# Moving table columns, scalings, sines and FFT pieces within the steps of a fused FFN and spectral-gate gradient kernel

## The chip, the core and the metric

The kernel runs on one core of a Trainium2 chip. The metric is the time of one execution on the device, in microseconds. A core has five engines that run their own instruction queues side by side and wait for each other through semaphores: TensorE (PE in the profile; its weight loads are shown as PEld), VectorE (DVE), ScalarE (ACT), GpSimd (POOL) and SyncE (SP, which here only issues DMAs). TensorE writes its sums to PSUM, and VectorE or ScalarE copies them out.

## The reference

The forward pass mixes two branches with a gate; the kernel computes its output and all gradients.

```python
def _fwd_reference(A_x, A_w_r, A_w_i, B_x, B_w_gate, B_w_up, B_w_down, gate_w):
    def _A_ref(x, w_r, w_i):            # x: 1 x 2048 x 576
        X = rfft2(x); X = X * (w_r + 1j * w_i)
        return irfft2(X, s=(2048, 576)).astype(bfloat16)
    def _B_ref(x, w_gate, w_up, w_down):  # 576 -> 4608 -> 576
        return (_gelu(x @ w_gate) * (x @ w_up)) @ w_down
    x = A_x
    g = _sigmoid((x * gate_w).sum(-1, keepdims=True))
    return g * _A_ref(x, A_w_r, A_w_i) + (1 - g) * _B_ref(x, B_w_gate, B_w_up, B_w_down)

def reference(A_x, A_w_r, A_w_i, B_w_gate, B_w_up, B_w_down, gate_w, B_x, grad_out):
    _out, _vjp = jax.vjp(_f, A_x, A_w_r, A_w_i, B_w_gate, B_w_up, B_w_down, gate_w)
    return (_out, *_vjp(grad_out))
```

(The FFT calls are shown shortened, and `_f` is the forward pass with `B_x` held fixed.) The eight outputs are the mixed output, the gradient of x, of the two spectral weights, of the three FFN weights and of the gate's weights. Inputs and outputs are bf16.

## The kernel before

The kernel has two phases. The first is a loop over 18 groups g of 256 hidden features, each with four steps m of 512 of the 2048 rows; step number pr = 4g + m runs from 0 to 71. The second phase (L1151 and around it) multiplies the stored hidden activations and gradients with the FFN weights.

A step of the first phase does this:

- **H work.** `H_mm` computes z (the output's gradient times w_down, L402 and L407), then the gate and up products xy (L411, L418) in two halves; `fft_next` may be called inside the second half, after 11 of its 16 matmuls. ScalarE scales z into da (`H_da`, L430) and copies each half of xy out three ways (`H_act`: xb L439, hu L440, q L437). VectorE does three operations in `H_ew1` (L445 to L447). Then `sigs`, which is `H_ew2`, does two sigmoids on ScalarE (om L461, s L462) and eight operations on VectorE (L466 to L473), whose results are A, dHg and dHu. The sigmoids of the four steps of group 0 are held over and issued in the next step (`held`).
- **W work**, the weight gradients of the group before (`W_units`): pieces called tail (L544, 32 half-width matmuls), dwd (L508) and dw (L527) accumulate in one of two PSUM banks of pool pw, and each ends with a copy (L486) to an output tile by `wcopy`, either on ScalarE (AC) or on VectorE (VC). In step 4 the first parts of two dw pieces run; in step 5 their second parts, the tail and one dwd; in step 7 one dw in four jobs. The dwd pieces read dB, the output's gradient, after it has been scaled in place by 1 - g (`scale_dB`, L952, eight rows of tiles in step 4 and eight in step 5).
- **FFT pieces.** The spectral branch is cut into a list of pieces that `fft_next` takes in order: u1 (L574), u2 (L591), then `tail_table` and `turned` (L608 to L633), s2 (L683), s1 (L772), z, ztail and d of the inverse (L818, L830, L844 and L846). `want` says how many pieces a step takes: none in steps 0 to 5, three in step 6, two in step 7, then one to five. The first goes between the two parts of xy, the others between the W jobs at the places in `spots`. Each piece's matmuls go to the pool pz, which holds one buffer and is shared with z; a ScalarE copy takes them out.

Each engine executes its queue in the order in which the program issues. The FFT needs tables: D (`build_D`), R (`build_R`, four calls for four parts) and B (`columns_B`, `build_B`). VectorE and GpSimd make the arguments; the sines are put in the list `tb.late` and `run_late` issues them on ScalarE, where the sine and sigmoid functions need different tables, so each batch has two table loads around it. Before the loop, tiles of the inputs are transposed on TensorE (`titems`, L367, L370, L373) into PSUM tiles of pool pg or ph, and copied out (L374) as dOT, wdT and xT. `gate` (L383, L385) makes g and 1 - g for a group of rows.

The lines of steps 4 to 71 that place this work:

```python
                if pr in (4, 5):
                    scale_dB(T // 2)
                if pr == 4:
                    build_R(nc, tb, unit, 4)
                elif pr == 5:
                    columns_B(nc, tb, res)
                    next(makeB)
...
                spots = (0.0, 1.6, 3.6) if n < 4 else (0.0, 1.0, 2.6, 4.2, 5.0, 5.0)
                tables = pr in (5, 7)
                for w, f in carry + hs:
                    if k < n and at >= spots[k - (n == 2)]:
...
                    if tables and k == n:
                        run_late(tb)
                        wcopy[0] = VC
```

Of the kernel before, what the change touches and what calls it, by code (L numbers as in the profile page):

```python
# [9 lines left out]
ACT = mybir.ActivationFunctionType  # L10
ALU = mybir.AluOpType
# [9 lines left out]
P, T = 128, 16  # L21
# [135 lines left out]
def build_R(nc, tb, unit, t0):  # L157

    V = nc.vector
    n = 4  # L160
    step = 2.0 * math.pi / S * EPS_SCALE
    X = unit([n, P], I32, name="XR")
    for t in range(n):
        V.scalar_tensor_tensor(X[:, t, :], tb.kk[:, 0, :], tb.scol[:, t0 + t:t0 + t + 1], tb.kk[:, 1, :], op0=ALU.mult, op1=ALU.add)
    V.tensor_single_scalar(X[:], X[:], S - 1, op=ALU.bitwise_and)
    if t0 % 8 == 0:
        tb.Rpair = unit([8, P], name="Rt")
    o = tb.Rpair[:, t0 % 8:t0 % 8 + n, :]

    tb.late.append(lambda: nc.scalar.activation(o, X[:], ACT.Sin, bias=tb.pi[:], scale=-step))  # L170
    tb.Rt += [tb.Rpair[:, t0 % 8 + t, :] for t in range(n)]
# [73 lines left out]
def kernel(  # L245
# [4 lines left out]
    nc = tc.nc  # L250
    LD = nc.sync
    ST = nc.gpsimd
    V = nc.vector
# [3 lines left out]
    res = ctx.enter_context(tc.tile_pool(name="res", bufs=1))  # L257
# [19 lines left out]
    xn = res.tile([P, T, D], BF16, name="xn")  # L277
# [8 lines left out]
    wts = {}  # L286
# [72 lines left out]
    def titems(src, dst, t0, ps, copies, n=4):  # L359

        def item(k, cs):
            def f():
                tp_ = ps[k](BF16).rearrange("p (j t m) -> p j t m", j=2, t=4)
                for j, c in enumerate(cs):
                    for tt in range(n):
                        if c < 4:
                            nc.tensor.transpose(tp_[:, j, tt, :], src[:, t0 + tt, eo(c)], ident[:])  # L367
                        elif n < 4:
                            for r in (LO, HI):
                                nc.tensor.transpose(tp_[r, 0, tt, :], src[:, t0 + tt, 512:D], ident[:])  # L370
                        else:
                            c0 = (t0 + tt) * D + (512, D - P)[tt % 2]
                            nc.tensor.transpose(tp_[:, 0, tt, :], src[:].rearrange("p t d -> p (t d)")[:, c0:c0 + P], ident[:])  # L373
                copies[k](dst[:, cs[0]:cs[0] + len(cs), t0:t0 + n, :], tp_[:, 0:len(cs), 0:n, :])  # L374
            return f
        return [item(k, cs) for k, cs in enumerate(((0, 1), (2, 3), (4,)))]
# [50 lines left out]
    def H_da(g, m, z):  # L427
        da = ewt("da", g)
        for t in range(4):
            nc.scalar.activation(da[:, t, :], z[:, t % 2, t // 2, :], ACT.Copy, scale=omg32[:, 4 * m + t:4 * m + t + 1])  # L430
        return da
# [450 lines left out]
    parity = iotas_R(nc, tb, res, unit)  # L882
    for f in titems(dB, dOT, 0, (pgtile, pgtile, phtile), (VC, AC, VC)):
        f()
    for f in titems(wdn, wts[0][1][:].rearrange("p k (c m) -> p k c m", c=2), 0, (phtile, pgtile, pgtile), (AC, VC, VC), n=2):
        f()
    for f in titems(xn, xT, 0, (pgtile, pgtile, pgtile), (VC, AC, VC)):
        f()
    D2[1]()
    D4[0]()  # L890
    D4[1]()
    parity()
    D4[2]()
    build_R(nc, tb, unit, 0)
    makeB = build_B(nc, tb, unit, res)

    fg = zipped(*fwd_units(xT, scr_x, None)) + zipped(*fwd_units(dOT, scr_g, gs32))
    ia, pa = inv_units(scr_p1, a_dv, SD2)
# [48 lines left out]
    carry, pend, held, rest = [], None, [], []  # L947
    scaled = [0]

    def scale_dB(n):  # L950
        for t in range(scaled[0], min(scaled[0] + n, T)):
            V.tensor_scalar(dB[:, t, :], dB[:, t, :], omg32[:, t:t + 1], None, op0=ALU.mult)  # L952
            scaled[0] = t + 1

    for g in range(NG):
        if g == 1:
            pgs.close()
            pw = ps1.enter_context(tc.tile_pool(name="pw", bufs=2, space=PSUM, **kw))
        for m in range(NPR):
            pr = g * NPR + m  # L960
            n = want(pr) - done[0]
            done[0] += n
            hs = [h for u in pend[m] for h in u] if pend else []

            def side_work(us):
                while side and us > 0:
                    us -= side[0][0]
                    side.pop(0)[1]()
            tiles = [ewt(tag, g) for tag in ("xb", "q", "hu")]
            state = []  # L970

            def sigs(g=g, m=m, tiles=tiles, state=state):
                H_ew2(g, m, tiles, state[0], state[1])
            if g == 0:
                def items(src, dst, t, *cp):
                    return titems(src, dst, 4 * t, (pgtile,) * 3, cp)
                head_, early, mid_, late_ = [
                    ([lambda: gate(0)], [], items(dB, dOT, 1, VC, VC, VC) + items(xn, xT, 1, VC, VC, VC) + items(dB, dOT, 2, AC, AC, VC), []),
                    ([], items(xn, xT, 2, VC, VC, VC), [], items(dB, dOT, 3, AC, AC, VC)),
                    ([], items(xn, xT, 3, VC, VC, VC), [], []),  # L980
                    ([], [], [], [])][m]
                if m == 1:
                    rest.append(late_.pop())
                elif m == 2:
                    head_ = [rest.pop()]
                z, xy_full = H_mm(g, m, head_)
                da = H_da(g, m, z)
                for f in early:
                    f()
                if held:  # L990
                    held.pop()()
                xy = xy_full(0)
                for f in mid_:
                    f()
                for part in (1, 0):
                    H_act(0, xy, tiles, part)
                xy = xy_full(1)
                for part in range(2):
                    H_act(1, xy, tiles, part)
                if m < NPR - 1:  # L1000
                    gate(m + 1)
                else:
                    V.tensor_copy(g32[:], g_bf[:])
                    V.tensor_scalar(gs32[:], g32[:], SD2, None, op0=ALU.mult)
                for f in late_:
                    f()
                state += [H_ew1(g, tiles), da]
                held.append(sigs)
            else:
                z, xy_full = H_mm(g, m)  # L1010
                xy = xy_full(0)
                da = H_da(g, m, z)
                for part in (1, 0):
                    H_act(0, xy, tiles, part)
                if held:
                    held.pop()()
                xy = xy_full(1, fft_next if n else None)
                for part in range(2):
                    H_act(1, xy, tiles, part)
                state += [H_ew1(g, tiles), da]  # L1020
                if pr in (4, 5):
                    scale_dB(T // 2)
                if pr == 4:
                    build_R(nc, tb, unit, 4)
                elif pr == 5:
                    columns_B(nc, tb, res)
                    next(makeB)
                elif pr == 6:
                    build_R(nc, tb, unit, 8)
                    next(makeB)  # L1030
                elif pr == 7:
                    build_R(nc, tb, unit, 12)
                side_work(4.4)
                at, k = 0.0, min(n, 1)
                spots = (0.0, 1.6, 3.6) if n < 4 else (0.0, 1.0, 2.6, 4.2, 5.0, 5.0)
                tables = pr in (5, 7)
                for w, f in carry + hs:
                    if k < n and at >= spots[k - (n == 2)]:
                        fft_next()
                        k += 1  # L1040
                    if tables and k == n:
                        run_late(tb)
                        wcopy[0] = VC
                        tables = False
                    if pr == NG * NPR - 1 and at == 0.0:
                        sigs()
                    f()
                    at += w
                wcopy[0] = AC
                while k < n:  # L1050
                    fft_next()
                    k += 1
                flush()
                if pr < NG * NPR - 1:
                    sigs()
            carry = []
            if m < 3 and g + 1 < NG:
                load_w(g + 1, m)
            if done[0] == n_slots or (pr >= wgT_from and pr % 2 == 0 and len(wgT_all) < 20):
                load_wgT()  # L1060
                if done[0] == n_slots:
                    load_wgT()
        carry = pend[4] if pend else []
        pend = W_units(g)
# [241 lines left out]
```

## Time and profile before

| what | value |
|---|---|
| time, median of 3 runs | 1425.34 us (1424.71 to 1425.42) |
| the profiled execution's own time | 1425.01 us |
| its span, first to last instruction | 1423.2 us |
| mean granted TensorE clock | 0.994 |
| PE busy | 1378.3 us, 97% |
| VectorE busy | 733.8 us, 52% |
| ScalarE busy | 729.9 us, 51% |
| GpSimd busy | 223.0 us, 16% |
| PE share of the chain that ended last | 91% |
| first phase (to the first L1151) | about 991 us |

All times within the execution count from its first instruction. In a timeline row stand the start, the length, the engine, the line, the operation, what it writes and reads, its shape and how many alike were merged; the bracket at the end holds the engine's idle time before it and what ended that. A length is that of one instruction as the profiler saw it, and the next may start some tenths of a microsecond before it ends, so rates are best read from start to start. In a row of waits stand the engine and what waited, what released it, the sum of idle time in us, the number of times and the longest one. The last matmul of a row ends by a model, so idle time of PE read from such rows is somewhat shorter than from the starts.

### The profile page before, as it was taken

The numbers are of one execution on the slowest core, as the hardware profiler recorded it, in microseconds if no ns is written. First come the engines' busy times: TensorE is split into PE (matmuls) and PEld (weight loads), VectorE is DVE, ScalarE is ACT, GpSimd is POOL, SyncE is SP. The second block draws the span as 40 slices with busy tenths as digits, with TensorE's granted clock in tenths as the row PEclk, the third lists the DMA queues.
The fourth block names the chain that finished last, engine by engine and source line by source line (L and its number), as shares of the span: only waits on it lengthen the run. The fifth ranks groups of instructions, "written<-read, shape, count | busy, mean of one in ns | idle before, by whom it ended". The sixth has DMA issues, their size and how long they took to land.

```text
span 1423.2 us, 28073 instructions
## 1 busy us (share of the span) xinstructions
PE 1378.3 (97%) x11357; PEld 1026.5 (72%) x11430; DVE 733.8 (52%) x1403; ACT 729.9 (51%) x1324; POOL 223.0 (16%) x420
## 2 busy tenths in 40 slices
PE   8879999999999999999999999999999999999997
PEld 6556767666776767667767767768777777777776
DVE  6866556464698778885565656551000642112100
ACT  6768777777788887776777776661000000000000
POOL 1020100112343533422100010110000100000000
PEclk9989999999999999999999999999999999999999
DMA  6334353435455664556356464759999997788773
GB/s 212 94 83 120 99 142 100 122 113 158 128 122 154 162 168 132 148 150 160 106 155 173 127 169 131 173 131 232 211 196 196 237 198 167 158 156 171 152 152 72
DMA packets 509534, 214.62 MB, mean 151 GB/s; under 512 B 311418, under 2 KB 502588, under 8 KB 509404
## 3 DMA queue, kind: packets, MB, share of 16 engines
q1 hardware_dynamic: 493402, 187.44, 56.4%
q0 software_dynamic: 13872, 24.24, 5.8%
q8 instruction: 89, 1.46, 0.4%
q10 hardware_dynamic: 2130, 1.15, 0.3%
q14 instruction: 41, 0.34, 0.1%
HBM read 41.05 MB, written 93.84 MB: 95 GB/s over the span
## 4 chain that ended last, share of the span: by engine, by line
PE 91%; ACT 4%; DVE 3%; issue 1%; DMA 0%; ACTq 0%; SPq 0%; DVEq 0%
PE acc L1151 30%; PE wps L527 16%; PE xy L418 15%; PE wps L508 10%; PE z L402 8%; PE wps L544 2%; PE xy L411 2%; PE pf L574 2%; PE z L407 1%; PE pf L844 1%; PE pf L683 1%; PE pf L846 1%; PE pf L591 1%; PE pf L818 1%; PE pf L772 1%
## 5 line engine op out<-in xcount | busy, mean ns | idle before, releaser
L1151 PEld LDWEIGHTS <-pin 128*128 128x128 bf16 x3456 | 338.0, 98 | 85.4 <-issue 0.2
L418 PE MATMUL xy<-wgu,xT 128*128 128x512 bf16 x1079 | 256.0, 379 | 9.9 <-issue 9.0
L527 PEld LDWEIGHTS <-xn 128*128 128x128 bf16 x2304 | 224.0, 98 | 34.8 <-issue 1.0
L418 PEld LDWEIGHTS <-xT 128*128 128x128 bf16 x1152 | 106.5, 98 | 137.8 <-issue 29.5
L1168 ACT COPY bo<-acc 128x288 f32<-128x288 f32 x32 | 12.7, 398 | 304.4 <-PE acc L1151 304.4
L466 DVE TENSOR_TENSOR xb<-xb,s 128x1024 bf16<-128x1024 bf16 x72 | 49.8, 692 | 222.6 <-ACT s L462 222.5
L508 PE MATMUL wps<-dB,A 128*128 128x288 bf16 x1152 | 154.9, 286 | 0.0
L1151 PE MATMUL acc<-wgT,pin 128*128 128x288 bf16 x1152 | 143.8, 286 | 0.0
L1151 PE MATMUL acc<-wuT,pin 128*128 128x288 bf16 x1152 | 143.6, 286 | 0.0
L1151 PE MATMUL acc<-wd_all,pin 128*128 128x288 bf16 x1152 | 142.6, 286 | 0.0
L402 PE MATMUL z<-wdT,dOT 128*128 128x256 bf16 x1152 | 137.5, 272 | 4.6 <-ACT ev L850 1.5
L527 PE MATMUL wps<-dHg,xn 128*128 128x256 bf16 x1152 | 136.2, 273 | 0.0
L527 PE MATMUL wps<-dHu,xn 128*128 128x256 bf16 x1152 | 135.2, 273 | 0.0
L508 PEld LDWEIGHTS <-A 128*128 128x128 bf16 x1152 | 112.2, 98 | 31.3 <-issue 0.4
L402 PEld LDWEIGHTS <-dOT 128*128 128x128 bf16 x1152 | 112.3, 98 | 20.9 <-issue 6.4
L430 ACT ACTIVATE da<-z,omg 128x256 bf16<-128x256 f32 x288 | 111.8, 470 | 13.6 <-PE z L407 10.4
L534 POOL DMA_DIRECT2D out_dram<-dw x67 | 49.4, 737 | 356.9 <-ACT dw L486 314.4
L1228 DVE SCALAR_TENSOR_TENSOR f32t<-gwf,dlog,b16t 128x576 f32<-128x576 f32 x16 | 13.1, 818 | 169.7 <-DMA b16t<-dxa_scr 169.7
L439 ACT CAST xb<-xy 128x512 bf16<-128x512 f32 x144 | 85.2, 592 | 26.8 <-PE xy L418 26.8
L437 ACT ACTIVATE q<-xy 128x512 bf16<-128x512 f32 x144 | 88.1, 614 | 6.8 <-PE xy L418 3.5
L486 ACT CAST dw<-wps 128x512 bf16<-128x512 f32 x69 | 40.4, 585 | 99.1 <-PE wps L527 91.9
L440 ACT CAST hu<-xy 128x512 bf16<-128x512 f32 x144 | 87.6, 608 | 0.0
(212 smaller groups left out, 1702.3 us busy)
## 6 DMA issues: line engine op xcount, KB each, us to landing
scr<-A SPq DMA_DIRECT2D x72, 256.0 KB, 2.4
scr<-dHg SPq DMA_DIRECT2D x72, 256.0 KB, 2.9
scr<-dHu SPq DMA_DIRECT2D x72, 256.0 KB, 3.5
out_dram<-dw POOLq DMA_DIRECT2D x67, 128.0 KB, 2.7
wd_all<-in_B_w_down_dram SPq DMA_DIRECT2D x3, 1728.0 KB, 9.9
out_dram<-dwd POOLq DMA_DIRECT2D x34, 144.0 KB, 2.8
scr_p<-Vt SPq DMA_DIRECT2D x32, 145.0 KB, 2.9
wgu<-in_B_w_gate_dram SPq DMA_DIRECT2D x18, 256.0 KB, 3.9
```

Source lines behind the costliest of these rows:

```text
L402: nc.tensor.matmul(zo(t), lhsT=dOT[:, ci, t, :], rhs=wdT[:, ci, :], start=(t % 4 < 2 and ci == 0), stop=False)
L418: nc.tensor.matmul(xy[k][:, t % 2, :], lhsT=xT[:, ci, t, :], rhs=wgu[:, ci, :], start=False, stop=(ci == 3))
L430: nc.scalar.activation(da[:, t, :], z[:, t % 2, t // 2, :], ACT.Copy, scale=omg32[:, 4 * m + t:4 * m + t + 1])
L437: nc.scalar.activation(q[:, h, :], xy[:, :, 0:FG], ACT.Square)
L439: nc.scalar.copy(xb[:, h, :], xy[:, :, 0:FG])
L440: nc.scalar.copy(hu[:, h, :], xy[:, :, FG:2 * FG])
L466: V.tensor_tensor(xb[:], xb[:], s[:], op=ALU.mult)
L486: wcopy[0](out, in_)
L508: nc.tensor.matmul(wps[:, :288], lhsT=tl(0, t)[:, fch * P:(fch + 1) * P], rhs=dB[:, t, h * 288:(h + 1) * 288], start=(t == 0), stop=(t == ...
L527: nc.tensor.matmul(wps[:, cc, :], lhsT=xn[:, t, (c0 + cc) * P:(c0 + cc + 1) * P], rhs=tl(k, t), start=(t == 0 and (cc == 0 or not both)), ...
L534: wst[0].dma_start(ov[:, c0:c0 + TPB, fsl], dw[:])
L1151: nc.tensor.matmul(acc[:, :288], lhsT=src[:, r, :], rhs=w_of(r)[:, h * 288:(h + 1) * 288], start=(first and r == 0), stop=(last and r == F ...
```

## The change

Six edits, all in the order of issue; the amount of computation stays the same.

1. **Opening.** The transposes of the first xn tiles, the rest of the D tables, `parity`, the first `build_R` and `gate(0)` become a function `opening` that is issued inside step 0's `H_mm`, behind the 16 z matmuls (L402). The third transpose item of wdn uses a ph tile instead of a pg tile. `makeB` is created ahead of it.
2. **Tables earlier.** `build_R(4)` moves from step 4 to step 0, `columns_B` from step 5 to step 0, and the first part of `build_B` (GpSimd iotas) from step 5 to step 1.
3. **Scaling.** The eight scalings of step 4 go to ScalarE; the eight of step 5 stay on VectorE.
4. **Held sigmoids.** In step 4 the sigmoids held over from step 3 are issued ahead of the first `H_act` instead of behind it.
5. **Sines behind W copies.** In step 5 `run_late` is issued ahead of job number 4 instead of ahead of the first job, so the copies of the two dw pieces come before it and stay on ScalarE; the tail's and the dwd's copies are on VectorE. In step 7 it is issued ahead of job number 1.
6. **Spread.** Piece k of a step's n FFT pieces is issued when k/n of the W work of the step, less 0.45 us, has been issued (or when as few jobs as pieces are left), instead of at the fixed places in `spots`.

```diff
--- before.py
+++ after.py
@@ -882,17 +882,20 @@
     parity = iotas_R(nc, tb, res, unit)
     for f in titems(dB, dOT, 0, (pgtile, pgtile, phtile), (VC, AC, VC)):
         f()
-    for f in titems(wdn, wts[0][1][:].rearrange("p k (c m) -> p k c m", c=2), 0, (phtile, pgtile, pgtile), (AC, VC, VC), n=2):
+    for f in titems(wdn, wts[0][1][:].rearrange("p k (c m) -> p k c m", c=2), 0, (phtile, pgtile, phtile), (AC, VC, VC), n=2):
         f()
-    for f in titems(xn, xT, 0, (pgtile, pgtile, pgtile), (VC, AC, VC)):
-        f()
-    D2[1]()
-    D4[0]()
-    D4[1]()
-    parity()
-    D4[2]()
-    build_R(nc, tb, unit, 0)
     makeB = build_B(nc, tb, unit, res)
+
+    def opening():
+        for f in titems(xn, xT, 0, (pgtile, pgtile, pgtile), (VC, AC, VC)):
+            f()
+        D2[1]()
+        D4[0]()
+        D4[1]()
+        parity()
+        D4[2]()
+        build_R(nc, tb, unit, 0)
+        gate(0)
 
     fg = zipped(*fwd_units(xT, scr_x, None)) + zipped(*fwd_units(dOT, scr_g, gs32))
     ia, pa = inv_units(scr_p1, a_dv, SD2)
@@ -947,9 +950,12 @@
     carry, pend, held, rest = [], None, [], []
     scaled = [0]
 
-    def scale_dB(n):
+    def scale_dB(n, on_act=False):
         for t in range(scaled[0], min(scaled[0] + n, T)):
-            V.tensor_scalar(dB[:, t, :], dB[:, t, :], omg32[:, t:t + 1], None, op0=ALU.mult)
+            if on_act:
+                nc.scalar.activation(dB[:, t, :], dB[:, t, :], ACT.Copy, scale=omg32[:, t:t + 1])
+            else:
+                V.tensor_scalar(dB[:, t, :], dB[:, t, :], omg32[:, t:t + 1], None, op0=ALU.mult)
             scaled[0] = t + 1
 
     for g in range(NG):
@@ -975,7 +981,8 @@
                 def items(src, dst, t, *cp):
                     return titems(src, dst, 4 * t, (pgtile,) * 3, cp)
                 head_, early, mid_, late_ = [
-                    ([lambda: gate(0)], [], items(dB, dOT, 1, VC, VC, VC) + items(xn, xT, 1, VC, VC, VC) + items(dB, dOT, 2, AC, AC, VC), []),
+                    ([opening], [], items(dB, dOT, 1, VC, VC, VC) + items(xn, xT, 1, VC, VC, VC)
+                     + [lambda: build_R(nc, tb, unit, 4)] + items(dB, dOT, 2, AC, AC, VC), []),
                     ([], items(xn, xT, 2, VC, VC, VC), [], items(dB, dOT, 3, AC, AC, VC)),
                     ([], items(xn, xT, 3, VC, VC, VC), [], []),
                     ([], [], [], [])][m]
@@ -992,6 +999,10 @@
                 xy = xy_full(0)
                 for f in mid_:
                     f()
+                if m == 0:
+                    columns_B(nc, tb, res)
+                elif m == 1:
+                    next(makeB)
                 for part in (1, 0):
                     H_act(0, xy, tiles, part)
                 xy = xy_full(1)
@@ -1010,38 +1021,35 @@
                 z, xy_full = H_mm(g, m)
                 xy = xy_full(0)
                 da = H_da(g, m, z)
+                if held:
+                    held.pop()()
                 for part in (1, 0):
                     H_act(0, xy, tiles, part)
-                if held:
-                    held.pop()()
                 xy = xy_full(1, fft_next if n else None)
                 for part in range(2):
                     H_act(1, xy, tiles, part)
                 state += [H_ew1(g, tiles), da]
-                if pr in (4, 5):
-                    scale_dB(T // 2)
                 if pr == 4:
-                    build_R(nc, tb, unit, 4)
+                    scale_dB(8, True)
                 elif pr == 5:
-                    columns_B(nc, tb, res)
-                    next(makeB)
+                    scale_dB(8)
                 elif pr == 6:
                     build_R(nc, tb, unit, 8)
                     next(makeB)
                 elif pr == 7:
                     build_R(nc, tb, unit, 12)
                 side_work(4.4)
+                jobs = carry + hs
+                total = sum(w for w, _ in jobs)
                 at, k = 0.0, min(n, 1)
-                spots = (0.0, 1.6, 3.6) if n < 4 else (0.0, 1.0, 2.6, 4.2, 5.0, 5.0)
-                tables = pr in (5, 7)
-                for w, f in carry + hs:
-                    if k < n and at >= spots[k - (n == 2)]:
+                tables = {5: 4, 7: 1}.get(pr)
+                for i, (w, f) in enumerate(jobs):
+                    if k < n and (at >= total * k / n - 0.45 or len(jobs) - i <= n - k):
                         fft_next()
                         k += 1
-                    if tables and k == n:
+                    if i == tables:
                         run_late(tb)
                         wcopy[0] = VC
-                        tables = False
                     if pr == NG * NPR - 1 and at == 0.0:
                         sigs()
                     f()
```

## The prediction, made before the changed kernel had run

> **What bounds the kernel now.** I read the page first: PE is busy 97% of the span and is 91% of the chain that ended last, so a change pays by what it takes out of PE's idle time, and the transfers, the weight loads and the second phase (L1151) need no look. The list of what PE waited for, read next, has one large line. The rows of 113 to 990 us, asked for alone, have a dozen small ones, of which three follow.
>
> ```profile
> PE wps L544 <- DVE dw L486: 11.0, 1, 11.0
> PE z L402 <- ACT ev L850: 1.5, 2, 0.8
> PE pf L772 <- ACT Xg L688: 1.0, 1, 1.0
> PE pf L683 <- ACT Xx L688: 1.0, 1, 1.0
> ```
>
> Third comes the timeline around the 11 us: PE, then VectorE, then the busy time by stretches: length, busy us of PE, weight loads, VectorE, ScalarE and POOL with counts, and behind POOL's the granted clock.
>
> ```profile
> 65.18 1.91 PE L527 MATMUL wps<-dHg,xn 128*128 128x256 bf16 x16
> 78.11 0.37 PE L544 MATMUL wps<-dHg,xn 128*64 128x256 bf16 x1 [11.02 <-DVE dw L486]
> ...
> 81.67 2.60 PE L508 MATMUL wps<-dB,A 128*128 128x288 bf16 x16
> 84.11 1.91 PE L402 MATMUL z<-wdT,dOT 128*128 128x256 bf16 x16
> ```
> ```profile
> 63.55 2.31 DVE L952 TENSOR_SCALAR dB<-dB,omg 128x576 bf16<-128x576 bf16 x8
> ...
> 73.94 2.32 DVE L952 TENSOR_SCALAR dB<-dB,omg 128x576 bf16<-128x576 bf16 x8
> ...
> 77.37 1.28 DVE L486 CAST dw<-wps 128x512 bf16<-128x512 f32 x2
> ```
> ```profile
> 67.10:72.40 5.30, 0.00 (x0) 0.03 (x1) 5.20 (x9) 3.72 (x7) 0.00 (x0) 1.00 0.34 102
> 72.40:78.10 5.70, 0.00 (x0) 0.00 (x0) 5.42 (x23) 5.14 (x6) 0.46 (x3) 0.50 0.62 150
> 78.10:82.70 4.60, 4.59 (x37) 3.85 (x37) 0.55 (x1) 0.00 (x0) 3.81 (x19) 0.50 0.01 4
> ```
>
> PE stands at step 5's tail piece (L544): both W banks hold finished sums, and their copies are queued on VectorE behind two scalings, the XR table, a full H_ew2 and the index columns. VectorE has no gap from 56.89 to 78.65; the chain of waits runs through it there. The stall is dearer than 11 us: the clock halves at 72.4 and comes back at 82.66, so the tail's 32 matmuls take 3.56 us from start to start where every later tail takes 1.87, and the next 16 take 2.44 for 1.96: 2.2 us more.
>
> **The change, part by part.** Durations are from the rows; times are before's clock.
>
> *Opening.* z (L402, 16 matmuls, 1.84 us) goes ahead of the xn transposes, and the last wdn transpose takes a ph bank. The 0.61 us wait at L370 goes (its ph bank is free from 6.82, so it ends at 7.16). What is late next: z's first matmul reads wdT, whose ScalarE copy (L374) ends at 7.97. So z starts at 8.03 and the xn transposes at 9.87, not 7.77. Before, z covered the copies of xT. Now the gate (L383) follows the transposes at once: the ScalarE copy ended 2.12 after the first transpose, so the gate starts at 12.05 and L407 at 12.65, where it stood at 11.72: 0.93 later. ScalarE and VectorE move by the full 2.1 us, since everything queued there stands behind the xT copies. VectorE's L165 then ends at 16.14, where PE's next transposes could be read at 15.79 and were read at 14.86. **+1.25 us** in all, on the chain, which runs through PE here. Bounds: 0 if later slack takes it up (the 0.78 us wait at 31.91 is itself in the chain), 1.6 if the table copies slip too. I take 1.25.
>
> *Tables in steps 0 and 1.* build_R(4) is 1.13 + 0.43 us on VectorE. It stands before a copy that began at 20.32 after 1.85 us of idle time, so it costs nothing; without that cover, 1.6. The columns are nine operations, 76.18 to 77.37, 1.2 us, ahead of L445 at 22.76, which had 2.02 of idle time before it: nothing. The POOL half (16 operations, 3.5 us, and five iotas, 1.7 us, by rows from 77.64 on) now runs beside VectorE. POOL's output queue holds nothing in these steps, so no DMA waits. Bounds: 0, and about 1 us, four times what the L136 pair lost beside POOL at 3.4 (0.89 us; 0.64 later). I take 0.
>
> *Steps 4 and 5.* ScalarE gets eight scalings that VectorE did in 2.31. The nearest row is the copy of almost the same width with a per-partition scale (L581, 128x580): 743 ns, of which about 0.11 overlaps the next (da lasts 470 and follows itself every 360 ns). 8 x 0.63 = 5.0 us. The Trainium skill speaks against this move: "ScalarE: Activation LUTs", Rules for kernel authors, puts multiplication on VectorE, up to three times faster there. The rows say 2.2 times. By the rule the eight stay: VectorE is free for step 4's H_ew2 at 65.2, the tail could start near 69.95 and z at 74.4, which would make the sum 0.9 us better than what follows. By the rows of the change ScalarE is the later one:
> - da(4) 51.80 to 53.24; om(3) must wait for s L446 (53.85); the two sigmoids now run first, to 56.0
> - six H_act copies at 0.48: 58.9; eight scalings: 63.9
> - om, s(4), 2.06: 66.0. They were free to start at 62.5, so the scaling delays them by 1.4
> - da(5) 1.44, six copies 2.9 (q waits for L468 until 68.3, just hidden): 70.4; first dw copy 0.59: 71.0
>
> The sines (table load 1.28, two sines 1.34, load 1.28) are now behind both W copies. So L544 starts at 71.0 instead of 78.11, a stall of 3.9. At the full clock its tail takes 1.87, to 72.9. The dwd piece (L508) needs dB's second half: H_ew2(4) on VectorE ends at 71.3, H_ew1(5) at 72.8, eight scalings at 75.1. Its last matmul therefore goes at 75.15, and z starts at 75.3 for 84.11: **-8.8 us**. da(6) then comes 2.3 us after z's start, as before (2.27), so nothing more is late. Bounds for one ScalarE scaling: 0.50 (width alone) to 0.74: the tail from 70.0 to 71.9.
>
> Here a second rule weighs. The clock stayed at 1.00 for 5.3 us after PE stopped. "TensorE: Matmul & The Clock Gate", Why this matters for your kernels, allows no gap over about 3 us. By the row a stall of 3.9 keeps the clock; by the rule it halves again and costs up to the 2.2 us. I take the row, with the rule as a rival.
>
> *Step 7.* The sines now stand after the first W job, ahead of the copy of step 7's second FFT piece (ve L594). ScalarE has its six copies done at 106.23; load and three table sines 3.03; the third needs XR at 108.72, so ve ends at 110.0. z (L402) shares that one-buffer PSUM pool and starts at 110.05 instead of 108.37. But step 8's first FFT piece waited for da until 114.90 anyway (1.2 us in the waits); 110.05 + 5.19 of PE work is 115.24: **+0.3 us**.
>
> *Spread of the FFT pieces.* z and every FFT piece share the one buffer of pz, so a piece too close behind the last waits for its copy. In the changed program's order 51 pieces move. The waits, with 0.16 us added to each because the view counts from a matmul's modelled end:
> - gone: four z right behind a piece (ev 1.5, ve 0.8, Y 0.7), five pieces 0.85 us of PE work behind an earlier one (Xg 1.0, Xx 1.0, Vt 0.8, and 0.4 put down to a DMA), two z behind Xx (0.8), one behind RT (0.2): 7.2 + 12 x 0.16 = 9.1
> - new: turned(1) comes 0.87 behind turned(0), whose copies are 0.37 and 1.02: 0.65. A second pair L818, L844 at 0.85 (0.39 where that stands now) and one at 0.96 (0.28), less a z behind ZT that goes (0.39)
>
> Net **-8.2 us**. Bounds -10 (new ones free) to -4 (half comes back as waits that no row shows).
>
> Sum: +1.25 - 8.8 + 0.3 - 8.2 = -15.45. The profiled execution took 1425.01 us (span 1423.2 and 1.8 around it); the median of the runs is 0.3 above. **1409.8 us.**
>
> **Rivals.**
> 1. The clock halves in the shorter stall, because what counts is where PE's pause falls in some fixed window. For: 3.9 us is more than the rule allows. Against: 5.3 us at full clock in this trace. 1409.8 + 2.2 = 1412.
> 2. The spread brings half: distances improve, but copies of pieces now queue behind W copies on ScalarE (7 tenths busy). For: most copies follow each other closely. Against: pairs now 1.75 us apart cost 0 to 0.2. 1409.8 + 4.2 = 1414.
> 3. The other side, slower: each of the 51 moved pieces delays a W copy on ScalarE and so one of the two W banks. Even with all old waits of this kind gone (12.8 us counted from starts), it takes over 0.45 us each to end above 1428; at turned's 0.65 it would be 1425 - 20 + 33 = 1438. Against: pieces already stand between W jobs in steps 8 to 23, and no wait of a W matmul on ScalarE is listed from 113 on.
> 4. The change does not free L544 because VectorE stays the late one, through q (L468). By the sums it is within 0.1 us of ScalarE's time, so a late H_ew2 costs at most its own delay: inside the range.
>
> **How the numbers follow.** Forecast with its bounds (1407 to 1412.9) 0.58; clock 0.15; half of the spread 0.15; slower 0.05; the rest, 0.07, is larger gains or a loss in an opening I misread. Ends of the range: all low bounds together, 1405; rivals 1 and 2 partly together, 1416. No change means within 0.2%, 2.9 us, about what this measurement can tell. Faster 0.92, same 0.03, slower 0.05.
>
> **What would show it.** Right: the wait at L544 is on ACT dw and near 3.9 us; no slice with clock under 1 in mid-kernel; the tail starting near 72.2 and z near 76.5 (the opening added); eight ScalarE scalings of about 720 ns; a gate wait of half a microsecond near 12; z waiting on ve once near 102; no L402 wait on ev, Y or Xx. Wrong: an L544 wait over 5 us, a halved clock, or new W waits on ACT.

## The result, and the profile after

The changed kernel takes **1411.49 us** (median of 4 runs, 1410.95 to 1411.9) against 1425.38 for the kernel before (4 runs, 1424.71 to 1425.42): a ratio of 0.9903, 95% interval 0.9886 to 0.9921. Its profiled execution took 1411.65 us, with a span of 1409.9. PE is busy 98% of the span and is 94% of the chain that ended last.

Where the 13.36 us between the two profiled executions went is read from the starts of z (L402), which divide the first phase into stages. All three columns are in us:

```
stage                                     before   after    predicted change
start to z of step 4                       46.82    48.11   +1.25
z of step 4 to z of step 6                 37.29    30.77   -8.8
z of step 6 to z of step 9                 39.10    39.48   +0.3
z of step 9 to the second phase (L1151)   867.42   858.82   -8.2
second phase, and time around the span    434.4    434.5     0
```

The differences are +1.29, -6.52, +0.38, -8.60 and +0.1. Three of the four edited stages came within 0.4 us; the second fell 2.3 short. The measured time is nearer to the 1412 of the prediction's rival 1 than to its own 1409.8.

The list of what PE waited for, steps 0 to 8 of the changed kernel (what waited, what released it, sum in us, times, longest):

```profile
PE wps L544 <- ACT dw L486: 4.1, 1, 4.1
PE z L402 <- ACT ve L594: 1.6, 1, 1.6
...
PE z L402 <- ACT wdT L374: 0.6, 1, 0.6
PE pf L383 <- ACT xT L374: 0.4, 1, 0.4
```

The 11.0 us at L544 are 4.1, and the engine named is now ScalarE. The two new small ones in the opening and the one at L594 stand where the prediction put them. From 113 us to the second phase the same list has two rows left where it had a dozen:

```profile
PE pf L630 <- ACT RT L636: 0.5, 1, 0.5
PE pf L844 <- ACT ZT L821: 0.5, 2, 0.2
```

Both are waits that the prediction listed as new. The list of before has one more row, `PE xy L418 <- issue: 8.3, 52, 0.2`, which is not idle time: in its rows of L418 one matmul of twelve is missing from the trace. g1_piece below shows the same 8.3 us and yet needs the changed kernel's time in that stage. The timeline of PE around the tail of step 5:

```profile
66.49 1.91 PE L527 MATMUL wps<-dHg,xn 128*128 128x256 bf16 x16
72.54 0.37 PE L544 MATMUL wps<-dHg,xn 128*64 128x256 bf16 x1 [4.13 <-ACT dw L486]
...
76.09 2.96 PE L508 MATMUL wps<-dB,A 128*128 128x288 bf16 x16
78.89 1.91 PE L402 MATMUL z<-wdT,dOT 128*128 128x256 bf16 x16
```

From start to start the tail takes 3.55 us, not 1.87, and the 16 L508 matmuls behind it 2.80. ScalarE, which released the tail:

```profile
60.11 5.48 ACT L956 ACTIVATE dB<-dB,omg 128x576 bf16<-128x576 bf16 x8
65.46 1.07 ACT L461 ACTIVATE om<-s 128x1024 bf16<-128x1024 bf16 x1
66.56 1.06 ACT L462 ACTIVATE s<-s 128x1024 bf16<-128x1024 bf16 x1
67.53 1.56 ACT L430 ACTIVATE da<-z,omg 128x256 bf16<-128x256 f32 x4
...
71.81 1.16 ACT L486 CAST dw<-wps 128x512 bf16<-128x512 f32 x2
72.99 1.28 ACT L170 ACT_TABLE_LOAD   x1
```

ScalarE has no gap from 60.11 on. The eight scalings take 5.35 us (60.11 to 65.46), 0.67 each from start to start; the sines and their table load follow the dw copies. Last, the busy time by stretches, cut where the clock changes (length; busy us of PE, weight loads, VectorE, ScalarE, POOL, with counts; granted clock; DMA):

```profile
67.57:70.98 3.41, 0.83 (x8) 0.60 (x7) 3.26 (x6) 3.41 (x10) 0.00 (x0) 1.00 0.31 85
70.98:74.39 3.41, 1.85 (x18) 1.85 (x19) 3.27 (x8) 3.38 (x7) 1.59 (x2) 0.50 0.41 121
74.39:77.80 3.41, 3.41 (x26) 2.40 (x22) 2.67 (x10) 3.38 (x4) 0.16 (x1) 0.50 0.77 210
77.80:81.20 3.40, 3.40 (x34) 2.64 (x32) 2.04 (x4) 1.29 (x3) 1.08 (x2) 1.00 0.46 97
```

The clock halves at 70.98, only 2.6 us after PE stopped (68.40), and stays so for 6.8 us, over all of the tail and most of L508. In the kernel before it had stayed at 1.00 for 5.3 us of pause. That is rival 1 of the prediction, and a halved clock was one of its signs of being wrong.

### The profile page after: what moved, and what is told of

It is laid out like the page before. It is cut to its first block, busy times and chain, and to the rows that moved or that the text cites. A ratio compares the mean times of both kernels' runs of the same rounds, so it can differ in the third digit from the quotient of the medians.

```text
span 1409.9 us, 28154 instructions
## 1 busy us (share of the span) xinstructions
PE 1387.4 (98%) x11430; PEld 1027.5 (73%) x11430; DVE 731.1 (52%) x1393; ACT 738.6 (52%) x1334; POOL 225.4 (16%) x420
## 4 chain that ended last, share of the span: by engine, by line
PE 94%; ACT 4%; DVE 1%; issue 0%; POOL 0%; POOLq 0%; DVEq 0%
PE acc L1159 30%; PE xy L418 17%; PE wps L527 17%; PE wps L508 10%; PE z L402 9%; PE wps L544 2%; PE xy L411 2%; PE pf L574 2%; PE z L407 2%; PE pf L844 1%; PE pf L772 1%; PE pf L591 1%; PE pf L846 1%; PE pf L818 1%; PE pf L683 1%; ACT q L437 0%
## 5 line engine op out<-in xcount | busy, mean ns | idle before, releaser
L418 PE MATMUL xy<-wgu,xT 128*128 128x512 bf16 x1152 | 270.2, 380 | 0.0
L418 PEld LDWEIGHTS <-xT 128*128 128x128 bf16 x1152 | 106.5, 98 | 137.8 <-issue 29.5
L508 PE MATMUL wps<-dB,A 128*128 128x288 bf16 x1152 | 154.7, 287 | 0.0
L402 PE MATMUL z<-wdT,dOT 128*128 128x256 bf16 x1152 | 137.5, 273 | 2.4 <-ACT ve L594 1.6
L508 PEld LDWEIGHTS <-A 128*128 128x128 bf16 x1152 | 112.4, 98 | 31.7 <-issue 0.4
L402 PEld LDWEIGHTS <-dOT 128*128 128x128 bf16 x1152 | 112.5, 98 | 17.1 <-issue 2.9
```

Source lines behind the costliest of these rows:

```text
L402: nc.tensor.matmul(zo(t), lhsT=dOT[:, ci, t, :], rhs=wdT[:, ci, :], start=(t % 4 < 2 and ci == 0), stop=False)
L418: nc.tensor.matmul(xy[k][:, t % 2, :], lhsT=xT[:, ci, t, :], rhs=wgu[:, ci, :], start=False, stop=(ci == 3))
L508: nc.tensor.matmul(wps[:, :288], lhsT=tl(0, t)[:, fch * P:(fch + 1) * P], rhs=dB[:, t, h * 288:(h + 1) * 288], start=(t == 0), stop=(t == ...
```

## Experiments

Two theories stood after this. Mine: each stage's difference belongs to the edit that the prediction gave it, and the shortfall in steps 4 and 5 is the halved clock. The rival: the shortfall is a queue (ScalarE or VectorE late for another reason), and the gains of the spread and of the opening are mixed up with each other. The first four kernels ran on one chip (kernel before there: 1426.92), the next four on a second (1425.58), the last four on a third (1426.24). Times of different chips are compared through their ratios. The stages of all the profiled executions, in us:

```
kernel              to z(4)  z(4)-z(6)  z(6)-z(9)  z(9)-2nd phase   span
before               46.82     37.29      39.10       867.42       1423.2
after                48.11     30.77      39.48       858.82       1409.9
e1_old_opening       47.06     30.75      39.47       858.71       1410.6
e2_warm_fill         47.90     28.68      39.47       858.70       1411.0
e3_scale_dve         47.95     27.54      39.47       858.71       1408.7
e4_before_spread     46.88     37.41      39.12       858.71       1417.6
f1_after_again       48.43     30.93      39.47       858.70       1410.5
f2_sines_only        47.39     30.42      42.36       867.42       1421.2
f3_open_dve          46.94     28.21      39.47       858.71       1406.0
f4_pool_scale        49.51     31.47      39.46       858.71       1412.4
g1_piece             46.83     27.54      38.77       858.71       1404.6
g2_piece_step7       47.40     27.53      38.42       858.72       1406.0
g3_held_old          46.92     29.23      39.48       858.72       1408.0
g4_sines_columns     47.34     31.89      39.11       867.45       1418.7
```

The first column holds the arrival of the first loads, which differs between executions by up to 0.6 us among the kernels with the same opening. From the z of step 1 to that of step 4 it is 24.47 us in all kernels but f4_pool_scale (26.60). The second phase, from its first L1151 (or what that line became) to the last instruction, also differs where no edit reaches it: 434.6 to 436.3 us in the profiles of the first chip and 432.6 to 433.9 in all the others. So a microsecond or two is better read from the stages than from the times.

### e1_old_opening: the opening alone

```diff
-                    ([opening], [], items(dB, dOT, 1, VC, VC, VC) + ...
+                    ([lambda: gate(0)], [], items(dB, dOT, 1, VC, VC, VC) + ...
```

The rest of edit 1 is undone in the same way.

> The changed kernel with edit 1 (the opening) undone, all else kept. My theory: the new opening costs 1.25 to 1.3 us on the chain of PE and nothing takes it up later, so this one takes 1410.2 us (1.3 less than the changed kernel's 1411.5), with z of step 1 (L402) back near 22.35. Rival, slack takes it up: 1411.5 us. The clock can shift the answer by up to 1 us either way, since PE's pause in step 5 then begins 1.3 us earlier.

Measured: 1411.9 us (1411.62 to 1412.36), ratio 0.9894 (0.988 to 0.9907). The first column loses 1.05, and every later stage is that of the changed kernel. The z of step 1 starts at 22.35 to 22.92 us in the ten profiles with the old opening and at 23.43 to 23.96 in the four with the new one. The ranges lie apart and their means by 1.0 us: that is what edit 1 costs, and the other 0.3 of the +1.29 is the arrival of the loads. The ratio is 1.3 us under the changed kernel's, but its interval overlaps that of the changed kernel, so the time alone does not prove it.

### e2_warm_fill: PE kept busy in the pause

This kernel adds 50 matmuls whose result nothing reads.

```diff
+                    if pr == 5 and i == 4:
+                        fill = pftile()
+                        for _ in range(50):
+                            nc.tensor.matmul(fill[:, 0, :P], lhsT=ident[:], rhs=ident[:], start=True, stop=True)
```

> The changed kernel with 50 matmuls of the identity, whose result nobody reads, put on PE in step 5 in front of the tail piece (2.8 us of PE work in its pause of 4.1 us, in the buffer of z and the FFT pieces). Theory (the halved clock is what the prediction lacked): the clock stays at 1, the tail's 32 matmuls take 1.87 instead of 3.56 us, z of step 6 starts near 76.75 (set by VectorE's last scaling of dB) instead of 78.9, and the kernel takes 1409.4 us. Rival (the pause itself and the scaling set z, and the clock only looks guilty): 1411.5 us.

The timeline of PE in it (L1053 is the fill):

```profile
68.89 2.95 PE L1053 MATMUL pf<-ident 128*128 128x128 bf16 x50 [0.71 <-ACT da L430]
72.29 0.27 PE L544 MATMUL wps<-dHg,xn 128*64 128x256 bf16 x1 [0.45 <-ACT dw L486]
74.16 2.57 PE L508 MATMUL wps<-dB,A 128*128 128x288 bf16 x16
76.57 1.91 PE L402 MATMUL z<-wdT,dOT 128*128 128x256 bf16 x16
```

Two stretches of it, over the pause and the tail (the granted clock stands third from the end):

```profile
69.01:72.42 3.41, 2.96 (x53) 2.89 (x53) 3.38 (x6) 3.41 (x8) 0.00 (x0) 1.00 0.29 82
72.42:75.83 3.41, 3.41 (x45) 2.83 (x43) 3.31 (x11) 3.36 (x5) 1.75 (x2) 1.00 0.60 168
```

The tail starts as late after z(4) as in the changed kernel (24.39 us for 24.43), but takes 1.87 us, and the clock never falls. z(4) to z(6) is 28.68, which is 2.09 less than in the changed kernel, and 0.2 from the 28.48 that the prediction had worked out for it (75.3 less 46.82). So the shortfall is the clock. The time was 1411.54 us (1410.53 to 1412.82), where 1409.4 was expected. Its ratio, 0.9891 (0.9878 to 0.9905), is 1.7 us under the changed kernel's, but the intervals overlap. In its profiled execution the second phase took 436.3 us, the longest of all, which ate the gain there; why was not tried.

### e3_scale_dve: all scalings on VectorE

```diff
                 if pr == 4:
-                    scale_dB(8, True)
+                    scale_dB(8)
```

> The changed kernel with edit 3 undone: step 4's eight scalings back on VectorE. Theory (ScalarE is the later engine of the two there, and the eight cost it 5.35 us): step 4's sigmoids start near 63.8 instead of 65.5, the tail (L544) near 71.1 instead of 72.5, z of step 6 between 75.4 and 77, so 1408.0 to 1409.6 us. Rival (the edit was right, VectorE cannot take them): a stall at L544 longer than 4.1 us and 1413 us or more.

Measured: 1411.62 us (1410.44 to 1411.88), ratio 0.989 (0.9876 to 0.9903). The pause falls to 2.64 us, the tail starts at 70.88 and the clock stays full, so z(4) to z(6) is 3.23 us shorter than the changed kernel's. The stretch that holds the start of the tail:

```profile
69.46:72.88 3.42, 2.00 (x33) 1.78 (x33) 3.28 (x6) 3.39 (x6) 1.71 (x2) 1.00 0.43 122
```

Set back by its later opening (47.95 for 46.82), the tail stands at 69.75 and z(6) at 74.36. The prediction had worked out 69.95 and 74.4 for just this, and then went by ScalarE's rows. Of the 3.23 us, 1.1 are the queue (28.68 in e2_warm_fill less 27.54, both at the full clock, for the 0.9 worked out) and 2.1 the clock behind the longer pause. The time missed the 1408.0 to 1409.6 expected. Only the profiled execution, the fastest (1410.44), had a mean clock of 0.998; the others had 0.996, 0.997 and 0.996. One window at half speed is 0.0012 of the span, so in those the clock most likely fell too, and the 3.23 is the good case.

### e4_before_spread: the spread alone

```diff
-                for w, f in carry + hs:
-                    if k < n and at >= spots[k - (n == 2)]:
+                jobs = carry + hs
+                total = sum(w for w, _ in jobs)
+                for i, (w, f) in enumerate(jobs):
+                    due = k < n and (at >= spots[k - (n == 2)] if pr < 8 else at >= total * k / n - 0.45 or len(jobs) - i <= n - k)
+                    if due:
```

> The kernel before with edit 6 alone, from step 8 on (the new places of the FFT pieces). Theory (pieces that share one PSUM buffer stood too close): 8.2 to 8.6 us less than before, 1416.9 us, and the waits of z on ev, Y and Xx gone. Rival (copies of moved pieces hold up W copies): half of it, 1421 us, with W matmuls waiting on ScalarE.

Measured: 1418.53 us (1418.33 to 1419.87, 5 runs), ratio 0.9941 (0.9928 to 0.9955). The fourth column is 858.71, and the three before it are within 0.12 us of those of before. The spread is worth 8.7 us of that stage and 8.4 of the median, and does not depend on the other edits.

### f1_after_again

> The changed kernel itself again, to stand beside the others on the same chip. Where the kernel before takes 1426.9 us, as on the chip of the first four experiments, this one takes 1413.1 us by the ratio 0.9903, and the first phase ends near 977 us again; what differs is in the second phase, whose first loads land later there.

Measured: 1412.0 us (1410.87 to 1412.49), ratio 0.9901 (0.9888 to 0.9915), with the clock halved for two windows again. It is the base for the second chip.

### f2_sines_only and g4_sines_columns: what the early columns are for

The kernel before, with step 5's sines moved and nothing else; then the same with the columns of B and its first iotas in steps 0 and 1.

```diff
-                for w, f in carry + hs:
+                for i, (w, f) in enumerate(carry + hs):
...
-                    if tables and k == n:
+                    if tables and k == n and (pr != 5 or i == 4):
```

> The kernel before with one piece of edit 5 alone: in step 5 the sines are issued ahead of job 4, so that ScalarE copies the two dw pieces first. Nothing else changes. Theory (the W copies' place in a queue is what cost, not VectorE's load as such): ScalarE has its last H_act copy done at 71.4, the tail (L544) starts near 72.0 instead of 78.1, z of step 6 between 76.4 (full clock) and 78.6 (halved) instead of 84.1; from z of step 4 to z of step 6 29.6 to 31.8 us, where before has 37.3 and the changed kernel 30.8. So this alone brings 5.5 to 7.7 us. Rival (edits 2 to 4 are needed to empty VectorE): 2 us or less.

> f2_sines_only (the kernel before with step 5's sines moved ahead of the fourth unit), with the small index columns of the tables made in the first two steps. Theory (in f2_sines_only GpSimd's 5 us of column arithmetic stands in its queue ahead of the stores of dw, and the next step's dW copies wait for these stores' buffers): z of step 6 to z of step 9 back at about 39.1 us instead of 42.4, z of step 4 to z of step 6 29 to 30.4, time some 3.3 us below f2_sines_only on the same chip, about 1418.5. Rival (the wait of the dW copies comes from the sines or from ScalarE itself): z6 to z9 stays near 42.

f2_sines_only took 1421.87 us (1420.82 to 1423.34, 8 runs), ratio 0.9973 (0.9963 to 0.9983). Moving the sines brings 6.9 us up to z(6), as expected, and then 3.3 go again in the next stage. The timelines of VectorE and of POOL in it:

```profile
77.88 0.17 DVE L182 CAST bcol<-bbit 128x4 f32<-128x4 int32 x1
85.78 0.42 DVE L486 CAST dwt<-wps 128x256 bf16<-128x256 f32 x1 [7.73 <-DMA out_dram<-dw]
```

```profile
78.22 0.35 POOL L186 TENSOR_SCALAR bcol<-bcol 128x1 f32<-128x1 f32 x2 [70.44 <-DVE bcol L182]
...
82.92 0.34 POOL L220 IOTA maskB<- 128x64 f32 x2
83.21 1.73 POOL L534 DMA_DIRECT2D out_dram<-dw  x2
```

dw's copies were done at 73.1 on ScalarE, but POOL issues their stores at 83.21, behind 5 us of small column arithmetic that waited for VectorE's columns. The tail's copy (dwt) needs a buffer that these stores give back, so VectorE stands for 7.7 us, and everything queued behind it with it. In g4_sines_columns the same copy runs at once:

```profile
76.96 0.41 DVE L486 CAST dwt<-wps 128x256 bf16<-128x256 f32 x1
```

and its third column is 39.11, so the cause is shown. Its time, 1420.29 us (1419.39 to 1421.34, 5 runs), ratio 0.996 (0.9947 to 0.9974), is better by less than expected, since z(4) to z(6) grew to 31.89. PE's pause is as long as in f2_sines_only, 4.98 us, and the tail starts as late. What differs is the window of the clock in which it starts, f2_sines_only first:

```profile
71.99:75.40 3.41, 2.76 (x27) 2.76 (x28) 3.27 (x9) 3.38 (x6) 0.00 (x0) 0.50 0.41 121
75.40:78.81 3.41, 3.41 (x35) 2.72 (x31) 2.48 (x15) 3.35 (x4) 0.59 (x4) 1.00 0.64 159
```

```profile
71.62:75.03 3.41, 2.43 (x24) 2.42 (x25) 3.27 (x8) 3.38 (x6) 1.72 (x2) 0.50 0.52 150
75.03:78.45 3.42, 3.42 (x22) 2.24 (x19) 2.35 (x9) 3.36 (x5) 0.77 (x2) 0.50 0.75 192
```

One window at half speed in the first, two in the second, and 1.5 us between them in that stage.

### f3_open_dve: without edits 1 and 3

> The changed kernel with edits 1 and 3 undone together (the old opening, all scalings on VectorE). Theory: the two add up: z of step 1 at 22.4 to 22.6, 27.5 us from z of step 4 to z of step 6, so the first phase ends 4.5 us earlier than the changed kernel's (near 972.6) and the time is 4 us under it on the same chip. Rival (they share one slack): 3 us or less.

Measured: **1407.63 us** (1407.4 to 1408.42), ratio 0.9873 (0.9859 to 0.9886). The changed kernel on the same chip took 1412.0, so these two edits cost 4.4 us together. The tail starts at 69.85, after a pause of 2.63 us, but here the clock did halve, for one window (69.46 to 72.88), and z(4) to z(6) is 28.21, not e3's 27.54:

```profile
69.46:72.88 3.42, 3.03 (x30) 3.03 (x31) 3.28 (x9) 3.39 (x5) 1.71 (x2) 0.50 0.51 138
```

### f4_pool_scale: the scalings on GpSimd

The old opening, and all 16 scalings on GpSimd in steps 2 and 3.

```diff
-                nc.scalar.activation(dB[:, t, :], dB[:, t, :], ACT.Copy, scale=omg32[:, t:t + 1])
+                nc.gpsimd.tensor_scalar(dB[:, t, :], dB[:, t, :], omg32[:, t:t + 1], None, op0=ALU.mult)
```

> As the one with the old opening, but all sixteen scalings of dB are issued on GpSimd in steps 2 and 3, where its queue holds nothing else. Theory (only the two late engines' load counts there): 1.0 us less than with VectorE, 26.5 us from z of step 4 to z of step 6, since the dwd piece no longer waits for the last scaling. Rival (GpSimd disturbs VectorE, which is full in steps 2 and 3): step 4's z comes 1 us or more later and the gain is gone.

Measured: 1414.39 us (1411.84 to 1414.44, 5 runs), ratio 0.9915 (0.9901 to 0.9929). The groups by line, of this kernel from 20 to 62 us and then two rows of it from 28 to 50 (busy us, mean ns, idle before):

```profile
L953 POOL TENSOR_SCALAR dB<-dB,omg 128x576 bf16<-128x576 bf16 x16 | 31.2, 1968 | 0.0
```

```profile
L468 DVE TENSOR_TENSOR om<-om,q 128x1024 bf16<-128x1024 bf16 x2 | 2.2, 1116 | 0.1
L445 DVE TENSOR_SCALAR s<-q 128x1024 bf16<-128x1024 bf16 x2 | 1.6, 797 | 0.0
```

In the changed kernel L468 takes 692 ns there and L445 419. The scalings run past the start of step 4, and these operations of VectorE take 1.6 and 1.9 times as long beside them (others, like L467 with 691 ns, do not), so step 4 starts 2.1 us late. z(4) to z(6) is 31.47 us where 26.5 was expected, with two windows at half speed. The rival was right.

### g1_piece and g2_piece_step7: useful work in the pause

f3_open_dve with the first FFT piece in step 5's pause; then also step 7's sines and second piece in their old places.

```diff
-    FIRST = (0, 0, 0, 0, 0, 0, 3, 5)
+    FIRST = (0, 0, 0, 0, 0, 1, 3, 5)
...
-                tables = {5: 4, 7: 1}.get(pr)
+                tables = {5: 4, 7: 0}.get(pr)
```

> f3_open_dve (the changed kernel with the old opening and all scalings on VectorE), with the first transform piece u1(0) issued in step 5's pause, ahead of the tail, instead of in step 6. Theory (the pause that is left there is worth its length and the clock behind it): the piece, 0.75 us of matmuls, fills a part of a pause of 2.6 us, the tail starts where it did (it waits for ScalarE's dw copies and the scalings), steps 6 to 9 lose 0.75 us (z of step 6 to z of step 9 38.7 instead of 39.47) and the clock is perhaps kept over the tail (z of step 4 to z of step 6 27.5 instead of 28.2): first phase 0.75 to 1.4 us shorter than in f3_open_dve, time about 0.5 to 1.4 us below it on the same chip, some 1406 to 1407. Rival (the piece's copy on ScalarE and its issue push dw and the tail out): z4 to z6 longer by 0.5 to 0.8, and no gain.

> g1_piece with step 7's own sines and second piece in the order of the kernel before (sines at the second unit, not behind W copies). Theory (the late sines cost 0.36 us there, a wait of 1.6 us on ScalarE against one of 1.2): z of step 6 to z of step 9 0.3 to 0.4 us shorter than in g1_piece, the rest the same. Rival (the 0.36 came from the pieces, not from the sines): no difference.

g1_piece: 1407.05 us (1406.39 to 1407.75), ratio 0.9868 (0.9854 to 0.9881). g2_piece_step7: **1406.9 us** (1406.45 to 1407.81), ratio 0.9867 (0.9854 to 0.9881). Both beat the kernel before and the changed one; against f3_open_dve, and against each other, the times do not decide, but the stages do. PE in g2_piece_step7:

```profile
67.51 0.91 PE L574 MATMUL pf<-Dt,xT 128*128 128x290 bf16 x6
70.31 0.27 PE L544 MATMUL wps<-dHg,xn 128*64 128x256 bf16 x1 [1.90 <-ACT dw L486]
...
74.93 1.91 PE L402 MATMUL z<-wdT,dOT 128*128 128x256 bf16 x16
```

The piece stands in the pause, and the clock stays at 1.00 over the tail in both kernels. In g1_piece, whose tail starts at 69.75:

```profile
69.00:72.40 3.40, 2.65 (x39) 2.30 (x39) 3.26 (x7) 3.37 (x6) 1.72 (x2) 1.00 0.54 153
```

Against f3_open_dve z(4) to z(6) is 0.67 us shorter (the clock), z(6) to z(9) 0.70 (the piece), and in g2_piece_step7 0.35 more. That 0.35 belongs to step 7's sines and second piece together; what each brings was not tried.

### g3_held_old: without edit 4

```diff
-                if held:
-                    held.pop()()
                 for part in (1, 0):
                     H_act(0, xy, tiles, part)
+                if held:
+                    held.pop()()
```

> f3_open_dve without the part that takes the held-back sigmoids of step 4 ahead of the first activation. Theory (ScalarE's queue sets the tail of step 5, so 0.8 us of it moved is 0.8 us of tail): z of step 4 to z of step 6 0.6 to 1.0 us longer than in f3_open_dve, and the time with it. Rival (the sigmoids are done long ahead of what waits for them either way): within 0.2 us of f3_open_dve.

Measured: 1409.57 us (1409.35 to 1410.03), ratio 0.9886 (0.9872 to 0.9899). The tail is 0.8 us later than in f3_open_dve and z(4) to z(6) 1.02 longer, the difference being tail time at the halved clock. Edit 4 was cheap and useful.

## Why the prediction was right, and where it was not

- **Opening.** Right in its mechanism, with the gate's wait at 0.38 us and L407 at 12.77, and near in its size: +1.25 for about 1.0. That the two profiles differ by just 1.29 is partly luck with the arrival of the loads.
- **Tables early at no cost.** Right: z of step 1 to z of step 4 is 24.47 us with and without them. What I did not see is what they buy: I put them down as costing nothing, and never asked what POOL's queue would do to the stores if they stayed. f2_sines_only and g4_sines_columns show 3.25 us.
- **Steps 4 and 5.** Mechanism and releaser right: the tail waits for ScalarE's dw copy, 4.1 us for 3.9, and starts at 72.54, which is 71.25 without the later opening, for 71.0. The 0.25 is the scalings: 0.67 us each, not 0.63 (one alone lasts 806 ns, where the row taken for it lasts 743). The step that failed is "By the row a stall of 3.9 keeps the clock; by the rule it halves again and costs up to the 2.2 us. I take the row". It halved: 1.68 us in the tail and 0.4 in L508, so the prediction's 2.2 was right as the cost and its choice of the row was wrong. One pause in one trace was read as a threshold. e4_before_spread, whose steps 4 and 5 and whose pause of 11.0 us are those of before, halved the clock 2.1 us after PE stopped (67.16 to 69.29), where before kept it for 5.3. In the Trainium skill, "TensorE: Matmul & The Clock Gate", Why this matters for your kernels, had the safer advice with its limit of about 3 us; but the 2.63 us of f3_open_dve halved the clock as well, so that limit is not a safe bound here.
- **The choice of ScalarE.** The Trainium skill's rule ("ScalarE: Activation LUTs", Rules for kernel authors) spoke against edit 3, and these runs agree with it: eight scalings took 5.35 us on ScalarE and 2.32 on VectorE. My sum by it, 0.9 us better, was right for the queue (e3_scale_dve: tail and z within 0.2 us of it). With the clock behind it the edit lost 2.6 us (f3_open_dve) to 3.2 (e3_scale_dve).
- **Step 7.** Right: +0.38 for +0.3, with z's wait on ve (1.6 us) where it was put; g2_piece_step7 gets 0.35 back by undoing step 7's new order.
- **Spread.** Right: -8.60 for -8.2, and the waits that remain are those listed. e4_before_spread shows that it stands alone. Rivals 2 and 3 are out: no W matmul waits for ScalarE from 113 us on. Rival 4 is out as well, since L544 is released by ScalarE.
- **Sum.** -13.36 for -15.45. Of the 2.1 us, 2.3 are steps 4 and 5, the spread gave 0.4 back, and the small rest is in the other stages. The sum came out inside the forecast because the clock cost only 2.1 us.

## What to carry to other kernels

Before moving work to another engine to unload one queue, write out that other queue up to the same waiting matmul: here the helper became the late one, and behind the longer pause of PE the clock stood at half speed for two windows, where the shorter pause had one or none. Small work on an engine that also issues stores delays these stores, and so the buffers they give back. Where PE must pause, put a piece of independent work in the pause: it pays its own length and may keep the clock.

## What the runs showed of the hardware

The clock changes on a grid of 3.41 us that lies differently in each execution: it stood at half for 3.4 us in f3_open_dve, 6.8 in the changed kernel, 10.2 in the one before and 13.7 in e4_before_spread. PE's busy share in the window before the clock fell, and in the windows at half speed, from the same view by stretches:

```
kernel              pause us   window before   windows at half speed
g3_held_old           3.5          0%          100%
f2_sines_only         5.0          0%          81%
g4_sines_columns      5.0          0%          71%, 100%
f1_after_again        4.1         13%          67%, 100%
after                 4.1         24%          54%, 100%
e1_old_opening        4.1         25%          54%, 100%
f4_pool_scale         2.9         23%          92%
f3_open_dve           2.6         34%          89%
e4_before_spread     11.0         37%          0%, 0%, 39%, 100%
before               11.0          0%          0%, 33%, 100%
```

So a window with up to 37% of PE work let the clock fall here, and a window at half speed with 81% or more brought it back, while 71% did not. Between these the share alone does not tell: ahead of before's idle window stood one with 44% and the clock stayed, and in f4_pool_scale, whose step 4 has short pauses, it fell after one with 44% (51.45 to 54.87). A pause of 2.6 us halved it in f3_open_dve and did not in e3_scale_dve. What exactly the chip counts stays open.

A GpSimd scaling of 128x576 took 1968 ns, against 0.29 us on VectorE (2.32 for eight) and 0.67 on ScalarE, and slowed VectorE beside it.
